# Attention and expert kernel: fp32 pairs scaled after the product instead of before, and one pair's scores in split halves

## The chip, the cores and the metric

One NeuronCore of a Trainium2 chip runs the whole program. The metric is the device time of one execution in microseconds; the median over the timed runs is compared. Engines: PE multiplies matrices, DVE (VectorE), ACT (ScalarE) and POOL (GpSimd) do element-wise work, SP (SyncE) issues the DMAs.

## What is computed

```python
q_pool = q.reshape(B, H, S // 2, 2, D).mean(axis=3)        # B=4, H=8, S=1152, D=64
scores = (q_pool @ k^T) / sqrt(D);  scores -= max(scores)
attn = exp(scores);  attn = attn / (sum(attn) + 1e-9)
x = attn @ v                                                # then (2304, 512)
h = x @ w_in;  g = where(h > 0, h, exp(min(h, 0)) - 1)
out = g @ w_out                                             # w_in 512x2048, w_out 2048x512
```

All inputs and the output are fp32.

## The kernel before

There are four units, one per batch entry. A unit has four pairs of heads. A pair is prepared once (q rows summed in twos, q and k transposed) and then runs nine steps: four blocks of 128 pooled queries for each head of the pair, and one step of 64 queries of both heads. A step makes 128 x 1152 scores on PE, takes their negated maximum on DVE while evicting them from PSUM into a buffer `ep` (`biggest`, L938), exponentiates in place on ACT with the row sum as a by-product (`expo`, L944), and makes the sum's reciprocal (`recip` on DVE, L952 and L953, or `recip_pool` on POOL, L960 and L961). After every second step, and after the last, the product with v gives a tile of x: five tiles per pair.

The string `SPLIT` names how each pair is computed, one letter per pair.

- `s`: scores and probabilities are split into fp16 halves. `phi` (ACT or POOL) and `plo` (DVE) multiply the exponentials by the reciprocal as they split them, DMAs transpose both halves, and 54 fp16 matmuls make a tile of x (`pv_split`, L1068).
- `F`: all fp32. q and k are transposed on PE (`flip`, L598 and L600, evicted at L603), scores are fp32 matmuls (`plain_rows`, L888 and L894). The exponentials are multiplied by the reciprocal in place, one pass over 128 x 1152 (L964 on POOL, L967 on DVE or L970 on ACT), transposed on PE in nine blocks (L1023), copied from PSUM to `pT` in three pieces (L1033 on ACT or L1036 on DVE), and 18 fp32 matmuls make a tile of x (`pv`, L1056).
- `f`: probabilities as in `F`, scores as in `s`: q and k go through absolute sums (L633), a scale (L685 to L689), a high half (L639 or, on POOL, L497), a low half (L653 or L659) and DMA transposes (L696 to L708); scores are fp16 matmuls (`whole_rows` and `half_rows`, L909, L914, L923).

Before, unit 0 is `FFFf`, units 1 and 3 are `ssss`, unit 2 is `ssfs`: five pairs have fp32 probabilities, 45 steps and 25 tiles of x. A tile of x is copied out of PSUM by L1077 (ACT) or L1081 and L1083 (DVE).

The experts follow each unit in two groups of 256 and 320 tokens: x is split into fp16 halves, 12 matmuls per block of `w_in` (L1167), the activation on ACT, DVE and POOL (L1180 to L1229), 12 matmuls per block of `w_out` (L1248). The weights arrive as raw words, are decoded on DVE (L776 to L780), summed on ACT (L792), and split (`split`: high half L803 or L497, low half L806 on DVE or L812 with L497 on POOL). That work falls into the time of unit 0.

The order of all 2,717 tasks is written out: `ORDER` lists them with a letter for the engine (p, v, a, g, s for PE, DVE, ACT, POOL, SP), each engine runs its own in that order, and `SLOTS` says which buffer each takes. PSUM has one buffer `s` of three banks for scores and five one-bank buffers `r` for everything else. `ep` has four buffers, in unit 0 joined by those of `wo` that are not yet in use.

Of the kernel before, what the change touches and what calls it, by code (L numbers as in the profile page):

```python
# [37 lines left out]
34s 509g 510g 493p 494v 472v 460a 33v 432p 433v 482p 461g 515p 495a 496v 483v 513p 42p 321v 530p
314s 473a 531v 497g 375s 514a 516a 293a 43a 309s 21a 306v 40p 44p 484a 462a 46p 511p 41a 485v 512a
48s 500p 310s 567p 501a 47a 568v 308a 299s 498p 517p 499a 569a 519p 486g 311v 474p 520v 45a 38p  # L40
467p 502p 475a 39a 316v 476p 570g 554p 521a 518a 555v 522g 523g 503a 487p 491p 477a 468a 36p 478p
465p 49g 479v 543p 456p 532a 533v 492a 488a 524p 323a 466a 534g 544v 545a 312v 50s 489p 463p 318a
578p 52a 546v 547g 490v 504p 53a 37a 324s 457v 464v 579v 54p 591p 535p 556a 557g 313a 301v 55v 592v
525a 552p 571g 539p 550p 536a 553a 548p 19s 537p 615p 51s 540a 326v 480p 616v 602p 580a 303a 328a
538a 558v 505v 617a 549a 528p 529a 551v 481v 559p 581g 329v 560a 56g 603v 618v 57g 561p 562a 582g
526p 330p 563p 604a 628p 61a 527v 331v 332p 377v 629v 583p 541p 605v 333v 584v 593a 594v 652p 390v
653v 58s 371s 62g 334g 619a 574p 564a 622p 587p 542a 379a 575a 630a 624p 620p 585p 586a 654a 639p
625v 572p 621a 335v 365s 360s 59s 588v 63s 336a 576p 565p 577a 623a 640v 60s 626p 663p 655v 367v
373v 641a 595a 566a 627a 606a 600p 337v 656v 631g 632g 381s 66s 64s 601a 573a 635p 636a 596p 607p
# [1272 lines left out]
```

## Time and profile before

| | |
|---|---|
| median of 3 runs | 751.39 us (751.33 to 752.59) |
| the profiled execution | 749.68 us, its span 747.8 us |
| busy: PE, DVE, ACT, POOL | 97%, 83%, 78%, 48% of the span |
| granted TensorE clock | 0.999 |
| DMA queue with the transfers | 83% of 16 engines, 125.49 MB |

The span runs from the first to the last instruction; the execution's own time has what lies around it. Busy shares are averages over stages that differ: unit 0 with the weights up to some 160 us, a mixed stage, then attention of one unit beside the experts of the one before, and the last group of the experts alone.

### The profile page before, as it was taken

To read this page: it belongs to the slowest core of one execution; us is meant where nothing else is said; L and a number is where in the kernel's file an instruction comes from. 1 tells how busy PE (TensorE), PEld (TensorE's weight loads), DVE (VectorE), ACT (ScalarE), POOL (GpSimd) and SP (SyncE) were. 2 spreads that over 40 slices of the span, in tenths; PEclk is the share of its full clock that TensorE was granted. 3 is DMA by queue.
4 is the path that set the end of the run, shared out by engine and by line. 5 is a ranking of instruction groups with operands and counts; after the bars stand their busy time and mean duration, and the time that the engine had idled before them with its cause. 6 is when DMAs were issued, how large, how long until landed. Compare 5 with 4: busy or idle time off the path is not lost.

```text
span 747.8 us, 19687 instructions
## 1 busy us (share of the span) xinstructions
PE 722.1 (97%) x7900; PEld 479.3 (64%) x7900; DVE 623.8 (83%) x1077; ACT 583.6 (78%) x980; POOL 357.1 (48%) x404
## 2 busy tenths in 40 slices
PE   5999999998999999999999999999999999999997
PEld 3677776776556655685566566787566655865753
DVE  6999999999998879899888888999898879774340
ACT  3999999999889777787979778988868766753651
POOL 0145547457465646155363656444677431452330
PEclk9999999999999999999999999999999999999999
DMA  8754952749899999999999997899999999793001
GB/s 286 257 200 133 314 167 65 197 85 211 158 187 191 184 194 189 166 207 197 185 198 197 189 227 156 185 183 188 191 178 204 184 184 161 127 126 64 29 1 36
DMA packets 308299, 126.75 MB, mean 169 GB/s; under 512 B 282928, under 2 KB 284976, under 8 KB 308208
## 3 DMA queue, kind: packets, MB, share of 16 engines
q1 hardware_dynamic: 308208, 125.49, 83.0%
q8 instruction: 62, 1.02, 0.6%
q14 instruction: 29, 0.24, 0.1%
HBM read 45.09 MB, written 4.72 MB: 67 GB/s over the span
## 4 chain that ended last, share of the span: by engine, by line
PE 52%; DVE 5%; POOL 2%; issue 1%; ACT 1%; DMA 1%; SPq 0%; POOLq 0%; ACTq 0%; DVEq 0%
PE r L1248 17%; PE r L1167 17%; PE r L1068 7%; PE s L909 5%; PE s L923 3%; DVE ep L997 2%; PE r L1023 1%; PE r L1056 1%; DVE ep L938 1%; DMA pT<-ep 1%; PE s L914 1%; ACT ep L944 0%; DVE tmp L1203 0%; POOL hb L991 0%; DMA pT<-hb 0%
## 5 line engine op out<-in xcount | busy, mean ns | idle before, releaser
L1167 PE MATMUL r<-x,wi 128*128 128x256 f16 (+1 forms) x1536 | 197.9, 286 | 4.5 <-DVE tmp L1203 2.3
L944 ACT ACTIVATE ep<-ep,wk 128x1152 f32<-128x1152 f32 x137 | 171.4, 1252 | 31.3 <-DVE ep L938 30.2
L938 DVE TENSOR_SCALAR_CACHE_REDUCE ep<-s,sm 128x1152 f32<-128x1152 f32 x117 | 165.1, 1411 | 20.6 <-PE s L923 10.7
L1167 PEld LDWEIGHTS <-wi 128*128 128x128 f16 x1536 | 147.3, 98 | 47.9 <-issue 9.9
L1248 PE MATMUL r<-wo,g 128*128 128x512 f16 (+1 forms) x864 | 174.9, 380 | 0.2 <-POOL g L1221 0.2
L997 DVE SCALAR_TENSOR_TENSOR ep<-ep,wk,hb 128x1152 f16<-128x1152 f32 x99 | 145.7, 1475 | 9.4 <-ACT hb L994 5.0
L1248 PEld LDWEIGHTS <-g 128*128 128x128 f16 (+1 forms) x864 | 73.6, 100 | 83.3 <-issue 4.3
L991 POOL TENSOR_SCALAR hb<-ep,wk 128x1152 f16<-128x1152 f32 x47 | 64.5, 1373 | 63.8 <-DVE wk L953 35.1
L497 POOL TENSOR_SCALAR wk<-wk 128x1 f32<-128x1 f32 x72 | 28.6, 398 | 132.7 <-ACT ep L944 129.1
L1068 PEld LDWEIGHTS <-v 128*64 128x64 f16 x2970 | 77.9, 110 | 12.1 <-issue 11.3
L994 ACT ACTIVATE hb<-ep,wk 128x1152 f16<-128x1152 f32 x52 | 64.7, 1250 | 26.8 <-POOL wk L961 7.9
L1068 PE MATMUL r<-pT,v 128*64 128x128 f16 (+1 forms) x2970 | 85.0, 215 | 0.1
L909 PE MATMUL s<-kT,qT 128*128 128x512 f16 (+3 forms) x390 | 76.7, 327 | 3.1 <-DVE ep L938 3.1
L1221 POOL TENSOR_TENSOR g<-tmp,g 128x320 f16<-128x320 f32 (+1 forms) x61 | 67.5, 1114 | 20.3 <-ACT g L1217 19.2
L1203 DVE SCALAR_TENSOR_TENSOR tmp<-r,tmp 128x320 f32<-128x320 f32 (+1 forms) x96 | 52.3, 552 | 28.5 <-ACT tmp L1193 13.9
L1180 ACT ACTIVATE tmp<-r 128x320 f32<-128x320 f32 (+1 forms) x96 | 45.2, 478 | 32.0 <-PE r L1167 19.0
L1183 ACT ACTIVATE tmp<-tmp,us 128x320 f32<-128x320 f32 (+1 forms) x96 | 57.7, 610 | 1.7
L909 PEld LDWEIGHTS <-qT 128*128 128x128 f16 (+1 forms) x390 | 31.7, 100 | 33.8 <-issue 9.9
L1023 PE MATMUL r<-ident,ep 128*128 128x128 f32 x342 | 49.7, 281 | 2.6 <-POOL ep L964 1.5
L961 POOL TENSOR_TENSOR wk<-wk 128x1 f32<-128x1 f32 x72 | 46.0, 639 | 6.0
L1225 POOL TENSOR_SCALAR g<-tmp 128x320 f16<-128x320 f32 (+1 forms) x41 | 25.7, 631 | 46.5 <-DVE tmp L1203 26.6
L923 PE MATMUL s<-kT,qT 64*128 64x512 f16 (+1 forms) x260 | 45.9, 389 | 0.7 <-DVE ep L938 0.7
(152 smaller groups left out, 1075.5 us busy)
## 6 DMA issues: line engine op xcount, KB each, us to landing
k<-in_k_dram SPq DMA_DIRECT2D x16, 576.0 KB, 4.7
v<-in_v_dram SPq DMA_DIRECT2D x16, 576.0 KB, 4.6
q<-in_q_dram SPq DMA_DIRECT2D x16, 512.0 KB, 4.5
g<-in_moe_w_out_dram SPq DMA_DIRECT2D x16, 512.0 KB, 4.8
g<-in_moe_w_in_dram SPq DMA_DIRECT2D x14, 512.0 KB, 6.2
qT<-qT SPq DMA_DIRECT2D x39, 144.0 KB, 2.9
out_dram<-tmp SPq DMA_DIRECT2D x16, 256.0 KB, 3.1
pT<-hb SPq DMA_TRANSPOSE x99, 3.6
```

Source lines behind the costliest of these rows:

```text
L909: nc.tensor.matmul(s.ap[rows, c, 0:n], pr.qT.ap[:, 0, j, rows], keys[h][c], start=first[c], stop=not first[c] and c < 2, skip_group_check= ...
L923: nc.tensor.matmul(s.ap[rows, c, 0:512], pr.qT.ap[r, 1, j, rows], keys[h][c][r], start=first[c], stop=not first[c], skip_group_check=True,)
L938: nc.vector.tensor_scalar(e_(), s.ap.rearrange("p a b -> p (a b)")[:, 0:S], -0.5 / float(D) ** 0.5 if pr.plain else pr.sm.ap[:, 12:13], No ...
L944: nc.scalar.activation(out=e_(), in_=e_(), func=AF.Exp, bias=nm.ap[:, 0:1], scale=-1.0, accum_out=nm.ap[:, 1:2],)
L991: nc.gpsimd.tensor_scalar(hb.ap, e_(), nm.ap[:, 1:2], 1.0, op0=ALU.mult, op1=ALU.mult)
L994: nc.scalar.activation(out=hb.ap, in_=e_(), func=AF.Copy, scale=nm.ap[:, 1:2])
L997: nc.vector.scalar_tensor_tensor(out=e16(), in0=e_(), scalar=nm.ap[:, 1:2], in1=hb.ap, op0=ALU.mult, op1=ALU.subtract)
L1068: nc.tensor.matmul(half(h), pr.v16.ap[:, h, order[c], e], p, start=(j + c == 0), stop=(j == 2 and c == NCH - 1), skip_group_check=True,)
L1167: nc.tensor.matmul(hp.ap[:, f * n:(f + 1) * n], w_in16[g][:, a, c, (f0 + f) * 128:(f0 + f + 1) * 128], x16.ap[:, e, c, g0:g0 + n], start=( ...
L1183: nc.scalar.activation(out=en.ap[:, :m], in_=en.ap[:, :m], func=AF.Exp, scale=us.ap[:, 8:9])
L1221: nc.gpsimd.tensor_tensor(out=l, in0=gv, in1=h, op=ALU.subtract)
L1248: nc.tensor.matmul(op.ap[r0:r0 + tn, :], gt[qd].ap[:, a, fi, o:o + tn], w_out16(f // 2)[:, e, f % 2, :], start=(i < 128 // tn), stop=(i >= ...
```

## The change

In `F` and `f` pairs the pass that multiplies the exponentials by the reciprocal is gone; the transposes wait for the exponential alone. The reciprocals go into eight columns of their own (`rc`). After the product with v, two more fp32 matmuls per tile multiply the reciprocals, broadcast over 64 columns, with the identity, so that columns 128 onward of the same PSUM bank hold them along the free dimension. The tile of x is then made in two steps: the broadcast reciprocals are copied to the place of x (ACT or DVE), and DVE multiplies the product by them. The third pair of unit 0 (index 2, called the second pair with split scores) goes from `F` to `f`. `ORDER` (now 2,697 tasks) and `SLOTS` are made anew throughout; no two stretches of more than five tasks agree on any engine's list. The engine letters that differ in number, before to after: copies to `pT` ACT 104 to 116, DVE 31 to 19; weights' low halves DVE 14 to 10, POOL 2 to 6; activation's high halves (L1217, L1225) ACT 52 to 40, POOL 44 to 56; k's low halves POOL 4 to 6, DVE 9 to 8. Normalising passes before: ACT 22, POOL 20, DVE 3. Copies of the reciprocals after: ACT 17, DVE 8; copies of x in those pairs before: ACT 15, DVE 10.

```diff
...
-SPLIT = ("FFFf", "ssss", "ssfs", "ssss")
+SPLIT = ("FFff", "ssss", "ssfs", "ssss")
 
 
 class Port(float):
@@ -374,6 +375,7 @@
     pool("qT", 2, [128, 2, 9, 128], F16)
     pool("sm", 3, [128, 14], F32)
     plan.pool("nm", 5, lambda j: wk[:, 61 + 2 * j:63 + 2 * j])
+    plan.pool("rc", 8, lambda j: wk[:, 18 + j:19 + j])
     pool("ep", 4, [128, S], F32)
     pool("wo", NG // 2, [128, 4, 2, DM], F16)
     pool("pT", 2, [128, 2, NCH, 128], F32)
@@ -945,29 +947,25 @@
                 out=e_(), in_=e_(), func=AF.Exp, bias=nm.ap[:, 0:1], scale=-1.0, accum_out=nm.ap[:, 1:2],
             )
 
+        rc = nm if pr.split else plan.buf("rc")
+
         def recip():
+            d = nm.ap[:, 1:2]
             if pr.split:
-                ts(nc.vector, nm.ap[:, 1:2], nm.ap[:, 1:2], 2.0 ** -15, 1e-9 * 2.0 ** -15, op1=ALU.add)
+                ts(nc.vector, d, d, 2.0 ** -15, 1e-9 * 2.0 ** -15, op1=ALU.add)
+                nc.vector.reciprocal(d, d)
             else:
-                nc.vector.tensor_scalar(nm.ap[:, 1:2], nm.ap[:, 1:2], 1e-9, None, op0=ALU.add)
-            nc.vector.reciprocal(nm.ap[:, 1:2], nm.ap[:, 1:2])
+                nc.vector.tensor_scalar(d, d, 1e-9, None, op0=ALU.add)
+                nc.vector.reciprocal(rc.ap, d)
 
         def recip_pool():
             d = nm.ap[:, 1:2]
             if pr.split:
                 ts(nc.gpsimd, d, d, 2.0 ** -15, 1e-9 * 2.0 ** -15, op1=ALU.add)
+                nc.gpsimd.tensor_tensor(out=d, in0=d, in1=minus, op=ALU.pow)
             else:
                 ts(nc.gpsimd, d, d, 1e-9, 1.0, op0=ALU.add)
-            nc.gpsimd.tensor_tensor(out=d, in0=d, in1=minus, op=ALU.pow)
-
-        def norm_pool():
-            nc.gpsimd.tensor_scalar(e_(), e_(), nm.ap[:, 1:2], 1.0, op0=ALU.mult, op1=ALU.mult)
-
-        def norm_dve():
-            nc.vector.tensor_scalar(e_(), e_(), nm.ap[:, 1:2], None, op0=ALU.mult)
-
-        def norm_act():
-            nc.scalar.activation(out=e_(), in_=e_(), func=AF.Copy, scale=nm.ap[:, 1:2])
+                nc.gpsimd.tensor_tensor(out=rc.ap, in0=d, in1=minus, op=ALU.pow)
 
         n = 128 if st.h is not None else 64
         modes = ("row", "row") if pr.plain else ("full", "row")
@@ -976,12 +974,14 @@
                        modes=modes if st.h is not None else ("both" if pr.plain else "col", "both"))
         tm = plan.add("DVE", 1345.0, t0 - K("KM", u), biggest, [ts_] + pr.sc, [s, nm, ep] + ([pr.sm] if pr.sm else []), lag=45.0)
         te = plan.add("ACT", 1255.0, t0 - K("KE", u), expo, [tm], [nm, ep])
-        tr = plan.add("DVE", 262.0, t0 - K("KE", u), recip, [te], [nm], [("POOL", Port(200.0, 270.0), recip_pool)], lag=160.0)
+        tr = plan.add("DVE", 262.0, t0 - K("KE", u), recip, [te], [nm] if pr.split else [nm, rc], [("POOL", Port(200.0, 270.0), recip_pool)], lag=160.0)
         tr.pen = CFG["PENR"]
         if not st.h:
             pr.pT = plan.buf(*TTAGS[u.i])
-            pr.pt = []
-        pT = pr.pT
+            pr.pt, pr.rc, pr.rec = [], [], []
+        pr.rc.append(rc)
+        pr.rec.append(tr)
+        pT, rcs = pr.pT, pr.rc
         if pr.split:
             hb = plan.buf("hb")
             e16 = lambda: e_().bitcast(F16)[:, 0:S]
@@ -1012,10 +1012,6 @@
             pr.pt.append(plan.add("DMA", Move(1480.0, 1250.0, True), t0 - CFG["KC"], ptr(0), [th], [hb, pT], lag=450.0))
             pr.pt.append(plan.add("DMA", Move(1480.0, 1250.0, True), t0 - CFG["KC"], ptr(1), [tl], [ep, pT], lag=450.0))
         else:
-            th = plan.add("POOL", pol(S), t0 - K("KH", u), norm_pool, [tr], [ep, nm],
-                          [("DVE", Port(760.0), norm_dve), ("ACT", act(S), norm_act)])
-            th.pen = CFG["PENN"]
-
             for j in range(0, NCH, 3):
                 tp = plan.buf("r")
 
@@ -1035,7 +1031,7 @@
                 def out_dve(j=j, tp=tp):
                     nc.vector.tensor_copy(dst(j), tp.ap[:, 0:384])
 
-                tt = plan.add("PE", 335.0, t0 - K("KT", u) + j, turn, [th], [ep, tp, pT], lag=80.0)
+                tt = plan.add("PE", 335.0, t0 - K("KT", u) + j, turn, [te], [ep, tp, pT], lag=80.0)
                 tq = plan.add("ACT", 380.0, t0 - K("KL", u) + j, out_act, [tt], [tp, pT], [("DVE", 480.0, out_dve)])
                 tq.pen = CFG["PENT"]
                 pr.pt.append(tq)
@@ -1057,6 +1053,12 @@
                         half(h), pr.v32.ap[:, h, order[c]], p,
                         start=(c == 0), stop=(c == NCH - 1), skip_group_check=True,
                     )
+            for h in range(2):
+                cols = ident if st.h is not None else ident[:, 64 * h:64 * h + 64]
+                nc.tensor.matmul(
+                    x.ap[64 * h:64 * h + 64, 128:128 + n], rcs[h if st.h is not None else 0].ap.to_broadcast([128, 64]), cols,
+                    start=True, stop=True, skip_group_check=True,
+                )
 
         def pv_split():
             for j, (a, e) in enumerate(((0, 0), (0, 1), (1, 0))):
@@ -1074,19 +1076,30 @@
             return u.x32.ap[:, pr.p, st.t * 128:st.t * 128 + n]
 
         def xa():
-            nc.scalar.activation(out=xdst(), in_=x.ap[:, 0:n], func=AF.Copy, scale=pr.sm.ap[:, 13:14] if pr.split else 1.0)
+            nc.scalar.activation(out=xdst(), in_=x.ap[:, 0:n], func=AF.Copy, scale=pr.sm.ap[:, 13:14])
 
         def xb():
-            if pr.split:
-                nc.vector.tensor_scalar(xdst(), x.ap[:, 0:n], pr.sm.ap[:, 13:14], None, op0=ALU.mult)
-            else:
-                nc.vector.tensor_copy(xdst(), x.ap[:, 0:n])
+            nc.vector.tensor_scalar(xdst(), x.ap[:, 0:n], pr.sm.ap[:, 13:14], None, op0=ALU.mult)
+
+        def xmul():
+            nc.vector.tensor_tensor(out=xdst(), in0=x.ap[:, 0:n], in1=xdst(), op=ALU.mult)
+
+        def ra():
+            nc.scalar.activation(out=xdst(), in_=x.ap[:, 128:128 + n], func=AF.Copy)
+
+        def rb():
+            nc.vector.tensor_copy(xdst(), x.ap[:, 128:128 + n])
 
         vb = [pr.v16, pr.sm] if pr.split else [pr.v32]
-        tp = plan.add("PE", 27 * mm(n) + 25.0 if pr.split else 18 * (2.08 * n / 2.4 + 1.5), t0 + K("KV", u), pv_split if pr.split else pv,
-                      list(pr.pt) + pr.vdone, [x, pT, u.x32] + vb, modes=("col", "col"), lag=60.0)
-        u.xdone[0 if st.t < 2 else 1].append(plan.add("DVE", 230.0, t0 + K("KV", u) - K("KX", u), xb, [tp], [x, u.x32] + vb,
-                                                      [("ACT", 250.0, xa)]))
+        tp = plan.add("PE", 27 * mm(n) + 25.0 if pr.split else 18 * (2.08 * n / 2.4 + 1.5) + 1.7 * n, t0 + K("KV", u), pv_split if pr.split else pv,
+                      list(pr.pt) + pr.vdone + ([] if pr.split else pr.rec), [x, pT, u.x32] + vb + ([] if pr.split else rcs), modes=("col", "col"), lag=60.0)
+        kx, bx = t0 + K("KV", u) - K("KX", u), [x, u.x32] + vb
+        if pr.split:
+            tx = plan.add("DVE", 230.0, kx, xb, [tp], bx, [("ACT", 250.0, xa)])
+        else:
+            tb = plan.add("ACT", 250.0, kx, ra, [tp], bx, [("DVE", 230.0, rb)])
+            tx = plan.add("DVE", 250.0, kx, xmul, [tb], bx)
+        u.xdone[0 if st.t < 2 else 1].append(tx)
 
     for st in steps:
         plan.at = str(st.u.i)
```

## Rows read from the trace of the kernel before

**Rows 1.** Windows by stage: length, then busy time (instructions) of each engine.

```profile
core 0: us, PE busy (x) PEld busy (x) DVE busy (x) ACT busy (x) POOL busy (x), PEclk, DMA share, GB/s
...
20.00:160.00 140.00, 134.87 (x1384) 100.95 (x1382) 134.35 (x273) 134.99 (x253) 69.48 (x72) 1.00 0.57 175
160.00:310.00 150.00, 143.45 (x1649) 90.23 (x1645) 137.50 (x217) 122.97 (x196) 84.69 (x89) 1.00 1.03 185
310.00:692.00 382.00, 380.51 (x4468) 249.72 (x4467) 323.95 (x534) 294.22 (x475) 188.24 (x214) 1.00 0.97 177
```

**Rows 2.** The chain that ended last, its last pieces: start, length, what.

```profile
691.78 26.08 PE r L1167 x192
717.87 26.14 PE r L1248 x144
```

**Rows 3.** PE's waits from 20 to 160 us: total, times, longest.

```profile
PE r L1023 <- POOL ep L964: 1.5, 1, 1.5
PE s L888 <- DVE ep L938: 1.3, 1, 1.3
...
PE r L1167 <- DVE x L1083: 0.2, 1, 0.2
```

**Rows 4.** Timeline of PE in unit 0: start, length, what, count of records.

```profile
36.38 2.19 PE L1056 MATMUL r<-pT,v 128*64 128x128 f32 x36
38.50 1.13 PE L888 MATMUL s<-kT,qT 64*128 64x512 f32 x4
...
39.77 0.87 PE L1023 MATMUL r<-ident,ep 128*128 128x128 f32 x6
40.57 1.09 PE L600 MATMUL r<-ident,q 128*64 128x128 f32 x16
41.60 1.13 PE L888 MATMUL s<-kT,qT 64*128 64x512 f32 x4
...
42.88 0.44 PE L600 MATMUL r<-ident,k 128*64 128x128 f32 x4
43.15 1.26 PE L600 MATMUL r<-ident,q 128*64 128x128 f32 x20
44.34 0.87 PE L1023 MATMUL r<-ident,ep 128*128 128x128 f32 x6
```

**Rows 5.** Timeline of PE, one split step (L923 to L914), then the experts.

```profile
483.87 0.39 PE L923 MATMUL s<-kT,qT 64*128 64x512 f16 x2
...
484.75 2.78 PE L1167 MATMUL r<-x,wi 128*128 128x256 f16 x24
```

**Rows 6.** Groups by line: the normalising pass on three engines; busy us, mean ns.

```profile
L970 ACT ACTIVATE ep<-ep,wk 128x1152 f32<-128x1152 f32 x19 | 23.9, 1257 | 2.2 <-DVE wk L953 1.8
L964 POOL TENSOR_SCALAR ep<-ep,wk 128x1152 f32<-128x1152 f32 x17 | 22.2, 1305 | 12.1 <-ACT pT L1033 8.8 <-DVE wk L953 2.4
...
L967 DVE TENSOR_SCALAR ep<-ep,wk 128x1152 f32<-128x1152 f32 x2 | 1.6, 808 | 0.0
```

**Rows 7.** Groups by line: evictions and a weight's low half.

```profile
L1033 ACT ACTIVATE pT<-r 128x384 f32<-128x384 f32 x85 | 38.1, 493 | 2.9 <-PE r L1023 2.9
...
L1036 DVE COPY pT<-r 128x384 f32<-128x384 f32 x23 | 12.4, 549 | 0.3 <-PE r L1023 0.2
...
L806 DVE SCALAR_TENSOR_TENSOR wi<-wi,wk,wi 128x1024 f16<-128x1024 f32 x5 | 6.4, 1275 | 0.0
...
L1083 DVE COPY x<-r 128x128 f32<-128x128 f32 x10 | 2.8, 282 | 0.2 <-PE r L1056 0.2
```

**Rows 8.** Timeline of POOL near 295 us, two passes of one kind.

```profile
293.86 2.42 POOL L991 TENSOR_SCALAR hb<-ep,wk 128x1152 f16<-128x1152 f32 x1 [0.19 <-POOL wk L961]
...
297.82 1.23 POOL L991 TENSOR_SCALAR hb<-ep,wk 128x1152 f16<-128x1152 f32 x1 [0.64 <-DMA pT<-hb]
```

**Rows 9.** Timeline of DVE in the same stretch.

```profile
293.86 1.41 DVE L997 SCALAR_TENSOR_TENSOR ep<-ep,wk,hb 128x1152 f16<-128x1152 f32 x1
298.18 2.07 DVE L997 SCALAR_TENSOR_TENSOR ep<-ep,wk,hb 128x1152 f16<-128x1152 f32 x1
```

More of the change, by code (lines that the diff above doesn't have):

```diff
@@ L38 @@
[L38 to L49, printed above, removed]
@@ L186 @@
[L186 to L188 removed]
+2s 6p 7v 8p 0s 320s 305s 295s 9a 294s 1v 322v 12p 307v 13a 4p 420p 421v 5a 10p 11a 422a 423g 433p
+426p 427a 18s 297v 434v 289s 376s 296v 443p 444v 435a 428p 24p 25a 441p 14p 436g 429a 378v 410p
+319s 300s 325s 298a 411v 16s 445a 446g 291v 437p 438a 412a 466p 467v 451p 452a 327v 15a 418p 414p
@@ new lines @@
+1041v 1034g 1035v 1057v 1036s 1042a 1043v 1058a 1048p 145a 1059g 2032g 1049v 1037s 1011a 1028p
+1044s 143s 1066p 2010a 1060a 1061v 1050a 1051v 2011g 1052a 1067v 1045s 1062s 1029a 1054s 2036p
+1074p 1053v 1075v 2052v 1046p 1068a 2046p 1084p 1063s 1076a 1077v 1055s 2047p 2048p 1069g 1064p
+1070g 1072s 1078a 1906s 1080s 1071v 1085v 1092p 1079v 1073s 146a 1065v 1047a 1081s 2049a 1086a
+2053v 1087v 1088g 1090s 2037a 2038s 147p 2054p 2055v 2058a 2042p 2043a 2044s 1093v 2059v 1089v
+1102p 1091s 1094a 1095g 1096g 1103v 2056v 1098s 148v 1097v 1099s 2088p 2089a 2050v 2090a 1104a
@@ new lines @@
+2067p 1120p 2060p 149a 150v 151s 154a 2061a 1121v 155v 1105g 1106g 1107v 2051s 1138p 1139v 2062a
+2068a 2063a 2069a 1122a 2070g 159s 1082p 1100p 1108s 2071v 1123g 1124a 2057v 2064v 2065a 2091g
+2072g 1112p 1113v 2081p 1125v 1130p 2073g 1140a 1114a 2095p 1101v 1141v 2092v 2093a 1115v 1109s
+1126s 152s 1127s 161s 160v 2094v 1131v 1116a 1118s 156s 1083v 2066g 153s 1142g 1143v 2082a 2109p
+1110p 2096a 2083a 2084g 2097a 2098a 2085v 1117v 1111a 2110a 1148p 2111a 1132a 1133g 1149v 2099v
+1119s 1134g 2074p 2075a 2076a 2100g 2077g 2078v 2128v 1135v 1144s 162s 2102p 2122p 1166p 1167v
@@ new lines @@
+192v 1234a 2164p 1235v 2165a 2177g 2206p 2155a 1242a 2166a 1227s 1250a 2156v 2199p 2217v 2167v
+2168v 187v 2200a 2201a 2202v 2133v 1251v 2185p 2203v 1243g 1244g 2207a 2218a 1236s 2208a 2209a
+2219g 2210v 2192p 1245v 1237s 1258p 1252a 2144a 1259v 1238p 188s 194s 189s 1228p 2169a 2145a 2211a
+2212g 1229a 1253v 2186a 1239v 2187a 2170v 2193a 2194a 2146g 2204g 2205g 2147v 2148g 2188v 1266p
+1246s 2227p 1267v 2228a 1260a 2241p 2195g 2149g 2234p 2196v 2189v 2197a 2242a 1268a 1261g 1255s
+1254s 1276p 1247s 193s 2248p 1277v 1262g 2220p 1264s 1278a 2198g 2221a 2222a 1263v 2190g 2191v
@@ new lines @@
+1827p 2500a 1795g 2481s 2511p 1828v 1801a 2501v 2502a 1797s 1802g 1776v 1796v 2496v 1778s 1798s
+1829a 2512a 2513a 2504p 2514g 1830g 2503g 2505a 2506a 2532p 2519a 2507a 2508v 1803a 2515v 2525p
+1804v 1831a 2516g 1805s 2517g 2533a 1806s 1817p 1818v 2534a 2509g 1832v 2526a 2527a 2528g 1819a
+1779p 2510v 1833s 2520a 2521a 1780a 1781p 1782v 2529v 2546p 2547p 1820v 1821a 1834s 1835p 1822v
+1823s 1783a 1807p 2535v 2536v 1784g 1785a 1824s 1787s 1809p 2552p 2553p 1836a 2522v 1810v 2523a
+1811a 2539p 2487v 2537g 2540a 2530g 2531g 1812v 2538v 1808v 1813g 1815s 1814v 1816s 2541a 1786v
@@ new lines @@
+2524v 2542v 2548p 1788s 1825p 1826a 2559v 1789p 2543v 2544a 2545g 1790v 2558v 2554p 2560p 2561v
+2564a 2549p 2555p 2556a 2562v 2550a 2551s 2565v 2580p 2581a 2566p 2567a 2657p 2601p 2568a 2569g
+2570v 2571a 2557s 2563v 2582a 2587p 2583v 2584v 2602a 2603a 2572v 2585g 2586g 2588a 2589a 2590g
+2591v 2604g 2643p 2644a 2645a 2646a 2647v 2605v 2573p 2574a 2575a 2576g 2577v 2578g 2579v 2664p
+2665a 2636p 2666a 2592g 2593v 2606g 2607g 2615p 2637a 2667a 2668v 2638a 2594p 2639g 2640v 2648a
+2641g 2642g 2616a 2617a 2618g 2669a 2619v 2629p 2620g 2649g 2621v 2658a 2684p 2659a 2660v 2661v
```

266 lines of the change are left out of this document (122 added, 144 removed), and 84 rows, old and new, of the table SLOTS.

## The prediction

> **What bounds the kernel now.** I read the windows by stage first, because the busy shares of the whole span mix stages. From 310 us on PE is the bound: it is busy for 380.51 of 382 us, DVE for 323.95, and the 1.5 us left are all that any better order of the other engines could win there [rows 1]. The end of the chain says the same: the last group of the experts is 26.08 and 26.14 us of PE without a break [rows 2]; the change touches none of it. From 20 to 160 us it is different. PE is busy for 134.87, DVE for 134.35 and ACT for 134.99 of 140 us: three engines at 96%, so none of them alone is the bound, and a relief of one runs into the next within some 5 us. From 160 to 310 us PE has 6.55 us idle, DVE 12.5, ACT 27 [rows 1]. So outside the start the whole idle time of PE that a lighter DVE or ACT can give back is 5.1 + 6.6 = 11.7 us before 310 us, and 1.5 after. PE's waits in the first stretch name the work that the change removes only for 1.5 us (the normalising pass on POOL); 1.3 us more wait for the eviction of scores on a full DVE [rows 3].
>
> **The change on PE.** An fp32 score step runs from 41.60 to 42.88 us, 1.28 us; a split step from 483.87 to 484.75 us, 0.88 us [rows 4, 5]. Nine steps of the third pair: 9 x 0.40 = 3.6 us saved. Its transposes go too: q takes 1.03 us (40.57 to 41.60) and 1.19 us (43.15 to 44.34), k's odd block 0.27 us (42.88 to 43.15), and eight square blocks at 0.13 us (six took from 39.77 to 40.57) 1.1 us: 3.6 us [rows 4]. One small matmul for the absolute sums comes in, at most 0.2 us. So this pair costs PE 7.0 us less. The broadcast of the reciprocals is new. Its two fp32 matmuls per tile have the shape of one of the nine column pairs in the product with v, which take 36.38 to 38.50 us, 2.12 us, for nine: 0.236 us a tile, half of that for the tile of 64. It could be nothing only if PE stood idle there; it could be 0.5 us if the two matmuls ran one after the other. I take 0.236: same type, same halves of the array, nothing between them. A pair has four whole tiles and a half one, 1.06 us; four such pairs in unit 0 cost 4.25 us, the one in unit 2 1.06 us [rows 4]. PE: -7.0 + 4.25 = -2.75 us in unit 0, +1.06 later, **-1.7 us** in all. Because PE has no slack after 310 us, this term should reach the end almost whole; its bounds are -3 and +5 us (broadcasts at 0.5 us: 25 x 0.26 = 6.5 us more).
>
> **The change on DVE and ACT, unit 0.** 36 of the 45 normalising passes lie in unit 0, by the table's letters 17 on ACT, 16 on POOL and 3 on DVE, at 1.257, 1.305 and 0.808 us [rows 6]. What the new table makes of it on DVE, by counting letters against rows: passes -3 x 0.81 = -2.4; copies to pT 21 to 8, -13 x 0.549 = -7.1; weights' low halves 14 to 10, -4 x 1.275 = -5.1 [rows 6, 7]. Against that 20 multiplications of 128x128 out of PSUM. No row shows one; a copy of that size is 0.282 us, a copy three times as wide 0.549 [rows 7], and I take 0.33, near the like size: +6.6. The third pair's low half of q and the fourth's, which moves from POOL, are passes of half the width of a weight's: +2 x 0.7; its scale chain is five tiny operations, +0.9; one copy of x fewer, -0.3; two low halves of the activation and one sum of q move away, -2. Sum -7.4 us, between -5 (multiplications at 0.45) and -9. ACT: -17 x 1.257 + 13 x 0.493 = -15, three passes more for the third pair (some 3.2), six evictions of transposes less (some -2.9): about -15 us [rows 6, 7]. POOL loses 16 passes, 21 us, and gets weights' and k's low halves; it is half idle, 69.48 of 140 us [rows 1], so its own length costs nothing while nobody waits for its results. Besides, each of the 36 steps loses the reciprocal and a pass of 0.8 to 1.3 us between the exponential and the transposes, so its `ep` buffer comes free earlier.
>
> **What that is worth.** The relief of DVE and ACT can only turn into time through PE's idle 11.7 us. Bounds: 0, where PE is idle for other reasons, and 7.4, what the busiest of the two loses. I take 3.0: the 1.5 us that name the removed pass, the 1.3 us that wait for a full DVE and the 0.2 us that wait for its copy of x [rows 3]. It lies below the middle because the three engines are level and PE's own order fills the gaps between its waits. What is late next is PE itself, and behind it the experts' evictions. After 310 us I take nothing: unit 2 loses nine passes on ACT and POOL, neither of which PE waits for there.
>
> **Waits that it adds.** The product with v now also waits for the reciprocals, with all later matmuls behind it on PE. They come a step of transposes and three copies (3 x 0.493 us) earlier [rows 7], and that covers them. The multiplication waits on DVE for ACT's copy, with score evictions behind it; if the copy is late, DVE stands for it. SP gets five issues more for the third pair (two transposes, three moves), with loads behind them; those are asked for tens of microseconds ahead in the table, and I cost them at nothing. Should that cover be gone, the decoding of weights is late and DVE with it.
>
> **Sum.** -1.7 - 3.0 = -4.7 us. Made against the profiled execution, 749.68 us (span 747.8, 1.9 us around it), it gives 745.0; the median of the runs shown, 751.39, lies 1.7 us above that execution, so the forecast for the median is **746.7 us**.
>
> **Rivals.**
>
> *PE alone.* The relief stays hidden because PE's idle time has other causes: only -1.7 us, 749.7 us. For it: three engines level, and most of PE's waits name DVE's evictions of scores, of which there are as many as before. Against it: DVE itself gets shorter.
>
> *The whole relief.* In unit 0 DVE is the true pace and PE only looks busy; its 7.4 us pass through: -9.1 us, 742.3 us. For it: DVE at 96%, and PE's records hide small gaps. Against it: ACT and PE at 96% as well.
>
> *POOL and DVE hold each other up.* A POOL pass of 1.23 us took 2.42 us when it began together with a DVE pass over two SBUF inputs, and that DVE pass took 2.07 instead of 1.41 us when POOL had begun 0.36 us before it [rows 8, 9]: the later one stands still for as long as the other runs. The change puts six more low halves on POOL, two passes each. If each of the 12 passes costs DVE the 0.66 us seen, that is 7.9 us, the relief is gone, and what is left is -1.7 and a little for the removed waits in one direction and late POOL results in the other: 750.2 us, no change that can be measured. Against it: 16 normalising passes that could do the same leave POOL in unit 0. The Trainium skill (SBUF — State Buffer, Who interferes with whom) says that DVE with two SBUF inputs and a POOL instruction that reads SBUF exclude each other for a whole instruction; the trace agrees. By that rule alone, moving a low half from DVE to POOL wins nothing, and the sum would be this rival's.
>
> *PSUM banks (slower).* A tile of x now leaves its `r` bank in two steps on two engines. The bank is held for the multiplication, 0.33 us, for the hand-over, and for what DVE has in hand when the copy is done: half of a pass of 1.41 us [rows 9], together about 1.0 us more. There are five such banks, and the transposes, the expert matmuls and the products all need them. If PE waits 0.3 us of it per tile, 25 x 0.3 = 7.5 us: 746.7 + 7.5 = 754.2 us, slower. It decides from about (4.7 + 1.5) / 25 = 0.25 us per tile on. For it: PE fills a bank in 0.4 us with transposes, and DVE is full. Against it: in the first stretch PE waits for a copy of x out of its bank only once, for 0.2 us [rows 3], and the tables leave the planner free to put other work between.
>
> **How the numbers follow.** Forecast 0.40, PE alone 0.15, the whole relief 0.15, POOL against DVE 0.10, PSUM banks 0.20. A measurement of this kernel tells about 0.2% from no change, 1.5 us: below 749.9 us is faster, above 752.9 us slower. Faster: 0.40 + 0.15 + half of PE alone (it lies on the line) = 0.63. Same: the other half and most of POOL against DVE, 0.16. Slower: the banks and a rest, 0.21. The forecast's own range is 743.5 to 749.8 us. Eight in ten needs the other cases: down to 741.5, a little past the whole relief, up to 754.5, the price of the banks.
>
> **What the profile after would show.** PE's busy time about 2 us less, the broadcast at 0.24 us a tile, the third pair's steps at 0.88 us. DVE some 7 us and ACT some 15 us less busy before 310 us; windows from 20 to 160 us with DVE and ACT below 96% and PE at or above it. The first experts (L1167, L1248) of unit 0 two to five microseconds earlier, and the stage after 310 us as long as before. Wrong would be: PE waits for copies or multiplications of x, for banks, or for POOL's low halves of weights; SP waits that delay loads in the first 80 us; or PE idle after 310 us beyond 1.5 us, which new tables could bring anywhere.

## The result, and the profile after

The changed kernel takes **756.49 us** (median of 9 runs, 753.19 to 757.24), the kernel before 751.33 beside it (9 runs, 749.62 to 753.51): ratio 1.0062, 95% interval 1.0044 to 1.0081. It is slower by 5.2 us where I forecast 4.7 us faster; 756.49 lies above the top of my range, 754.5. The profiled execution took 757.17 us, its span 755.4. It lies 7.5 us above the profiled one before, more than the medians do, so the losses read from the two profiles below add up to more than 5.2 us.

Windows by stage after, to be held against [rows 1]; the last two lines look closer at two short stretches with PE alone:

```profile
20.00:160.00 140.00, 128.97 (x1367) 99.61 (x1366) 132.40 (x266) 120.46 (x243) 58.65 (x62) 0.96 0.62 181
160.00:310.00 150.00, 144.72 (x1629) 91.59 (x1627) 135.18 (x218) 121.28 (x191) 91.22 (x91) 1.00 0.99 179
310.00:692.00 382.00, 376.88 (x4515) 249.11 (x4514) 328.42 (x546) 280.38 (x459) 184.53 (x223) 1.00 0.98 179
...
104.00:120.00 16.00, 12.11 (x107) 0.79 0.25 92
140.00:155.00 15.00, 11.80 (x109) 0.89 0.25 75
```

ACT lost what I said (14.5 us in the first stage), POOL 10.8. DVE lost only 2.0 and PE is idle for 11.0 of 140 us instead of 5.1. The granted clock, 1.00 before, is 0.96: behind 104 and behind 140 us it fell to the lower of its two levels (1.2 instead of 2.4 GHz) for a while: 0.51 from 107 to 114 us, 0.50 from 144.6 to 148. After 310 us PE is idle for 5.1 us instead of 1.5. The fp32 products of unit 0 end at 171.0 us (before 166.8), those of unit 2 at 492.0 (483.9), the last split product at 691.5 (683.9): some 4 us are lost up to 171 us, some 4 between there and 492, nothing after.

PE's waits from 20 to 160 us after, against [rows 3]:

```profile
PE s L925 <- DVE ep L940: 4.7, 2, 3.9
PE r L1019 <- DVE x L1085: 3.2, 1, 3.2
PE s L890 <- DVE ep L940: 1.4, 2, 1.2
```

Two long waits, both for DVE, make up the new idle time. The first, in the timeline of DVE (L778, L779 and L782 are the three operations of a decoding, L940 the eviction of scores):

```profile
99.93 1.60 DVE L493 TENSOR_SCALAR sm<-sm 128x3 int32<-128x3 int32 x1
...
102.65 0.41 DVE L778 TENSOR_SCALAR tmp<-g 128x512 uint32<-128x512 uint32 x1
103.10 1.49 DVE L779 SCALAR_TENSOR_TENSOR tmp<-g,tmp 128x512 uint32<-128x512 uint32 x1
104.62 2.49 DVE L782 SCALAR_TENSOR_TENSOR wo<-g,tmp 128x512 uint32<-128x512 uint32 x1
107.04 1.41 DVE L940 TENSOR_SCALAR_CACHE_REDUCE ep<-s,sm 128x1152 f32<-128x1152 f32 x1
```

and in that of POOL and of PE:

```profile
99.36 2.15 POOL L814 TENSOR_TENSOR wi<-wi,wi 128x1024 f16<-128x1024 f32 x1
102.79 1.26 POOL L499 TENSOR_SCALAR wi<-wi,wk 128x1024 f32<-128x1024 f32 x1 [1.28 <-ACT wi L805]
104.13 2.44 POOL L814 TENSOR_TENSOR wi<-wi,wi 128x1024 f16<-128x1024 f32 x1
```

```profile
104.23 0.39 PE L1058 MATMUL r<-ident,wk 128*64 128x128 f32 x4
108.51 0.61 PE L925 MATMUL s<-kT,qT 64*128 64x512 f16 x2 [3.89 <-DVE ep L940]
```

The operation at 99.93 is three columns wide and takes 1.60 us; the one behind it of the same form takes 0.17. It ends when POOL's pass at 99.36 ends. The decoding's second and third operations take 1.49 and 2.49 us where 0.69 is usual, beside two more passes of POOL. These are low halves of the input weights. The new table moved the one at 99.36 to POOL; the one at 102.79 and 104.13 (task 341) ran on POOL before, too, and it is the new order that puts a decoding beside it. The eviction that PE needs is queued behind the decoding. The second wait has the same make-up: between 140.0 and 144.1 us a high half of v and a sum of q on POOL hold two decodings up, and the multiplication of a tile of x, whose bank PE wants, stands behind them:

```profile
140.01 1.23 POOL L499 TENSOR_SCALAR v<-v,sm 128x1152 f16<-128x1152 f32 x1 [2.85 <-PE r L1052]
140.19 1.60 DVE L782 SCALAR_TENSOR_TENSOR wo<-g,tmp 128x512 uint32<-128x512 uint32 x1
...
142.50 1.60 POOL L579 TENSOR_TENSOR q<-q 128x576 f32<-128x576 f32 x1
142.88 1.77 DVE L782 SCALAR_TENSOR_TENSOR g<-g,tmp 128x512 uint32<-128x512 uint32 x1
144.58 0.41 DVE L1085 TENSOR_TENSOR x<-r,x 128x128 f32<-128x128 f32 x2
```

The Trainium skill (SBUF — State Buffer, Who interferes with whom) says that of a DVE operation with two SBUF inputs and a POOL instruction that reads SBUF, the one that starts first keeps the shared ports for its whole instruction. The decodings at 103.10 and 104.62 agree: each began behind a pass of POOL and ended 0.54 us behind that pass's end.

To see how much DVE loses that way, I count its operations from 20 to 172 us that took over 0.4 us longer than the median of their line and shape in the same run, and call them held: three in the kernel before, 2.3 us too long in all; ten in the kernel after, 11.7 us. Beside each of them POOL had a pass in hand. Five of the ten, 6.2 us, lie beside low halves of weights, the other five beside POOL's passes on q, k, v and the probabilities.

### The profile page after: what moved, and what is told of

It is laid out like the page before. It is cut to its first block, busy times and chain, and to the rows that moved or that the text cites. A ratio compares the mean times of both kernels' runs of the same rounds, so it can differ in the third digit from the quotient of the medians.

```text
span 755.4 us, 19764 instructions
## 1 busy us (share of the span) xinstructions
PE 722.4 (96%) x7953; PEld 481.9 (64%) x7953; DVE 627.0 (83%) x1087; ACT 554.4 (73%) x952; POOL 354.8 (47%) x413
## 5 line engine op out<-in xcount | busy, mean ns | idle before, releaser
L940 DVE TENSOR_SCALAR_CACHE_REDUCE ep<-s,sm 128x1152 f32<-128x1152 f32 x123 | 173.7, 1412 | 23.4 <-PE s L925 15.0
L991 POOL TENSOR_SCALAR hb<-ep,wk 128x1152 f16<-128x1152 f32 x50 | 67.7, 1354 | 53.6 <-DVE wk L956 20.5
L499 POOL TENSOR_SCALAR wk<-wk 128x1 f32<-128x1 f32 x70 | 19.5, 279 | 154.9 <-ACT ep L946 151.1
L911 PE MATMUL s<-kT,qT 128*128 128x512 f16 (+3 forms) x420 | 83.1, 328 | 4.6 <-DVE ep L940 4.6
L1070 PEld LDWEIGHTS <-v 128*64 128x64 f16 x2970 | 77.8, 110 | 12.4 <-issue 11.7
L994 ACT ACTIVATE hb<-ep,wk 128x1152 f16<-128x1152 f32 x49 | 61.1, 1249 | 25.0 <-POOL wk L965 11.3
L1234 POOL TENSOR_TENSOR g<-tmp,g 128x320 f16<-128x320 f32 (+1 forms) x57 | 62.1, 1092 | 22.5 <-ACT g L1230 20.6
L911 PEld LDWEIGHTS <-qT 128*128 128x128 f16 (+1 forms) x420 | 33.9, 100 | 37.9 <-issue 15.0
L925 PE MATMUL s<-kT,qT 64*128 64x512 f16 (+1 forms) x280 | 49.6, 390 | 7.1 <-DVE ep L940 7.1
L1238 POOL TENSOR_SCALAR g<-tmp 128x320 f16<-128x320 f32 (+1 forms) x54 | 40.5, 754 | 32.5 <-DVE tmp L1216 28.6
L1201 POOL TENSOR_SCALAR tmp<-tmp,us 128x320 f32<-128x320 f32 (+1 forms) x39 | 29.9, 768 | 52.4 <-ACT tmp L1196 51.1
```

The lines of the kernel that those rows point to most:

```text
L911: nc.tensor.matmul(s.ap[rows, c, 0:n], pr.qT.ap[:, 0, j, rows], keys[h][c], start=first[c], stop=not first[c] and c < 2, skip_group_check= ...
L925: nc.tensor.matmul(s.ap[rows, c, 0:512], pr.qT.ap[r, 1, j, rows], keys[h][c][r], start=first[c], stop=not first[c], skip_group_check=True,)
L940: nc.vector.tensor_scalar(e_(), s.ap.rearrange("p a b -> p (a b)")[:, 0:S], -0.5 / float(D) ** 0.5 if pr.plain else pr.sm.ap[:, 12:13], No ...
L991: nc.gpsimd.tensor_scalar(hb.ap, e_(), nm.ap[:, 1:2], 1.0, op0=ALU.mult, op1=ALU.mult)
L994: nc.scalar.activation(out=hb.ap, in_=e_(), func=AF.Copy, scale=nm.ap[:, 1:2])
L1070: nc.tensor.matmul(half(h), pr.v16.ap[:, h, order[c], e], p, start=(j + c == 0), stop=(j == 2 and c == NCH - 1), skip_group_check=True,)
```

## The experiments

All were timed in five rounds, each beside the kernel before on the same chip (its medians: 750.07 to 751.52 us). Where two kernels of different experiments are compared I take the difference of their ratios to the kernel before, times 750 us, with the root of the sum of the squared half intervals as its uncertainty; by its ratio the kernel after stands at +4.7 us. Line numbers of the experiments differ by up to two from those of the kernel they come from. In ORDER, a number is a task, the letter its engine.

**1. Low halves back on DVE, decodings later, both** (from the kernel after).

```diff
-335g 339g 341g 345g 347g        # e1: low halves of five blocks of w_in
+335v 339v 341v 345v 347v
-357v 387v ... 770v              # e2: two decodings behind a multiplication of x; e3: both edits
+770v 357v 387v
```

> The changed kernel with the five low halves of w_in that POOL makes put back on DVE, at the same places of the list. Theory A (POOL's low halves hold DVE up; PE then stands still and its clock falls): the long DVE passes between 99 and 107 us are gone, with them PE's wait of 3.9 us at 104.6 us and the stretch of half clock behind it (5.4 us of work at half speed, 2.7 us lost): some 5 to 7 us less than the changed kernel, 749 to 751 us, although DVE gets 5 x 1.27 = 6.4 us of work of its own. Theory B (the tile of x made in two steps, with its PSUM bank held, costs the time): no gain, or slower by what DVE gets, 756 to 760 us.

> The changed kernel with two multiplications of x (third pair) put ahead of two weight decodings on DVE's list; nothing else moves. Theory B: PE's wait of 3.2 us at 145 us for the bank that such a multiplication frees is gone, and 3.2 us at half clock behind it (1.6 us lost): 4 to 5 us less, about 752 us. Theory A: DVE is late there because POOL held two of its decodings up (1.60 and 1.77 instead of 0.69 us), so the wait moves to the next user of DVE; at most 1 us less, 755 to 757 us.

> Both edits. If the two stalls are separate, their gains add: 10 to 12 us less than the changed kernel, 745 to 747 us, under the kernel before. If they are one (DVE late all along), the sum is no more than the larger one: 749 to 752 us. Theory C (what is lost after 310 us by the new order, some 3.5 us, is a third cause): not below 747 us.

Measured: 756.18, 757.29 and 755.05 us (ratios 1.0060, 1.0078 and 1.0051; each interval holds 1.0062). In e1 the operations at 99 to 107 us run at their usual length and DVE's held time falls from 11.7 to 5.4 us, but the five low halves (one of them had been on POOL before the change) cost DVE as much, 5 x 1.275 us, and PE stands for 3.8 us at the second place, not 3.2. In e2 PE's second wait becomes one of 4.0 us for a score eviction. Both together win 0.8 us (uncertain by 1.8); a wait of 3.7 us at 146 us is left. So a stall removed by more work on DVE comes back at the next user of a late DVE.

**2. The mirror: four more low halves on POOL in the kernel before.**

```diff
-335v 339v 345v 347v
+335g 339g 345g 347g
```

> The kernel before, with four of the low halves of w_in that DVE makes put on POOL at the same places (six of eight then run there). Theory A: DVE loses 5.1 us of work but stands still for POOL's passes, and late weights come on top: 2 to 8 us slower, 753 to 759 us. Theory B, and the step of the forecast that counted the move as a relief of DVE: same or up to 3 us faster, 748 to 752 us.

Measured 757.82 us, ratio 1.0084 (1.0067 to 1.0102): 6.3 us slower, with this one part of the new table, in the old order. DVE's decodings from 20 to 172 us, in this run:

```profile
L776 DVE SCALAR_TENSOR_TENSOR tmp<-g,tmp 128x512 uint32<-128x512 uint32 x26 | 22.4, 862 | 0.9
...
L779 DVE SCALAR_TENSOR_TENSOR wo<-g,tmp 128x512 uint32<-128x512 uint32 x14 | 11.4, 814 | 0.5
```

in the kernel before:

```profile
L777 DVE SCALAR_TENSOR_TENSOR tmp<-g,tmp 128x512 uint32<-128x512 uint32 x27 | 19.5, 724 | 0.9
...
L780 DVE SCALAR_TENSOR_TENSOR wo<-g,tmp 128x512 uint32<-128x512 uint32 x14 | 9.7, 692 | 0.5
```

and in the kernel after:

```profile
L782 DVE SCALAR_TENSOR_TENSOR wo<-g,tmp 128x512 uint32<-128x512 uint32 x14 | 13.2, 943 | 0.5
...
L782 DVE SCALAR_TENSOR_TENSOR g<-g,tmp 128x512 uint32<-128x512 uint32 x2 | 2.5, 1230 | 0.1
```

The same operations on the same data sizes: 26 x 0.138 + 14 x 0.122 = 5.3 us longer in e8, and 14 x 0.251 + 2 x 0.54 = 4.6 us longer in the kernel after. About as much DVE time is lost there as the move was to save (5.1 us). With DVE's other operations, e8 has eleven held ones, 9.1 us, 6.9 more than before: the move costs DVE more than it saves.

**3. The change on the order of the kernel before.** e4 moves the scaling and nothing else, e5 also moves 16 copies to `pT` from DVE to ACT, e6 is the whole change, e7 is e6 with e5's move.

```diff
-... recip, norm, turn ...    pv, x (a or v)
+... recip, turn ...          pv, xr (a or v; e5, e7: v), xmul v
```

> The kernel before with the scaling moved and nothing else: its order of tasks, its engines and its third pair in whole fp32; the 45 normalising passes are left out, each fp32 tile of x gets the broadcast, the copy of the reciprocals on the engine that copied x before, and the multiplication on DVE right behind it. PE: 20 whole and 5 half broadcasts at 0.31 and 0.16 us, +7.0 us. DVE in unit 0: 20 multiplications at 0.28 and 3 passes of 0.81 fewer, +3.2 us. New tables guilty: this order has few late score evictions, so only PE's 7 us less some idle time that goes away: 756 to 758 us. Scaling itself guilty (the two-step way out of the bank holds up PE in any order, 0.2 us a tile more): 761 us or more, with PE waits on the multiplication of x of over 4 us between 20 and 160 us. Forecast's own terms (broadcast 0.236, relief 3): 754.

> As e4_scale_only, but the copies of the reciprocals on DVE and 16 copies to pT of unit 0 moved from DVE to ACT, which lost 17 passes: DVE's sum in unit 0 falls by 16 x 0.55 less the copies that came to it. If a full DVE is what holds PE up in unit 0: 2 to 4 us faster than e4_scale_only. If the bank is what holds PE (the copy and the multiplication now follow each other on one engine, so without a hand-over): also faster, and PE's waits on x near 0 in both. If PE alone sets the time: equal to e4_scale_only within 1 us.

> The whole change on the order of the kernel before: moved scaling as in e4_scale_only, and the third pair with split scores, its new tasks put where the old flips stood. New tables guilty: e4_scale_only less the third pair's 7 us of PE, give or take 2 for DVE's two more passes: 749 to 753 us, 3 to 7 us faster than the kernel after. Structure guilty, in any order: 755 to 758 us, as the kernel after.

> The whole change on the order of the kernel before, with the copies of the reciprocals on DVE and 16 copies to pT of unit 0 moved from DVE to ACT. New tables guilty and DVE the pace of unit 0: the forecast's relief shows here, 746 to 750 us, faster than the kernel before. Structure guilty: 754 us or more. PE alone the bound: equal to e6_before_order within 1 us.

Measured: 765.87, 767.68, 772.38 and 776.58 us (ratios 1.0193, 1.0219, 1.0286 and 1.0337), 8 us (e4) to 27 us (e7) above what the theory of guilty tables gave, and in e4 without the waits on the multiplication that the other one asked for. In e4 DVE is busy for only 126.47 us of the first stage's 140, and PE is idle for 9.4; 5.3 us of its waits name late score evictions. A lighter DVE alone won nothing in this order, which was written for other lengths, and moving 16 copies off it made it no better (e5 against e4 2.0 us slower, uncertain by 2.5; e7 against e6 3.8 by 2.8). The third pair's change made it 7.0 us slower here (e6 against e4), where PE was to save as much; PE waits 3.1 us there for one absolute sum of q that ACT makes, so this says little of the new order, in which no run tests the third pair alone. So "the new tables are to blame, the old order would do better" falls: the new tables serve the change far better than the old order does. What hurts in them has to be looked for inside the new order.

**4. What PE's broadcasts cost.** e9 makes them in 16 bits, e11 issues them twice.

```diff
-rcs[h ...].ap.to_broadcast([128, 64]), cols
+rcs[h ...].ap.bitcast(BF16)[:, 1:2].to_broadcast([128, 64]), cols      # e9, cols likewise
-for h in range(2):
+for h in (0, 1, 0, 1):                                               # e11
```

> The kernel after with the broadcast's two matmuls in 16 bits: they read the upper 16 bits of the reciprocal and of the identity, so each reciprocal is cut to 8 bits of mantissa; order, engines, waits and every other instruction as they were. A broadcast took 0.31 us in fp32; in 16 bits I expect about a quarter, 0.08. If PE sets the time wherever the broadcasts lie: 25 tiles x 0.2 = 5 us less, 751.5 us, as fast as the kernel before. If late DVE work sets the pace of unit 0 and of unit 2's pair: PE arrives earlier and waits longer, 755 to 756.5 us.

> The kernel after with the broadcast's two matmuls issued twice into the same place, nothing else. If PE sets the time: 25 more broadcasts at 0.28 to 0.31 us, +7 us, 763.5 us. If PE's idle time in unit 0 and in unit 2's pair takes them in: +1 to +3 us, 758 to 759.5 us.

Measured: e9 755.51 us (ratio 1.0077, 1.0057 to 1.0096), no faster than the kernel after (1.1 us slower, uncertain by 2.0), with a broadcast at 0.16 us (100.64 to 100.80 us) instead of 0.32 and the granted clock in the two short stretches as in the kernel after; e11 **753.32** (1.0044, 1.0029 to 1.0059), where +7 or +1 to +3 us were expected: 25 more broadcasts cost nothing, and the middle value is 1.4 us lower (uncertain by 1.8). Less work on PE wins nothing at the same clock, and more costs nothing, so the amount of PE's work isn't the pace of unit 0. In e11 the second broadcasts shorten the two waits to 3.2 and 1.5 us (the one at 104.23 us above is the last thing PE does before the first), and the granted clock from 104 to 120 us is 0.89 instead of 0.79, from 140 to 155 us 1.00 instead of 0.89. That suggests that the clock gives back what the work costs.

**5. That reading tested: PE kept busy in the two stalls only.**

```diff
-for h in range(2):
+for h in (0, 1) * (8 if (u.i, pr.p) == (0, 2) and st.t in (0, 4) else 1):
```

> The kernel after with two tiles' broadcasts issued eight times into the same place: the whole tile that ends at 104.6 us, right ahead of PE's 3.9 us of waiting, and the tile of 64 that ends at 139.9, three tasks ahead of the 3.2 us. PE gets 7 x 0.31 + 7 x 0.16 = 3.3 us more to do, all in place of standing idle. If the half clock behind the two stalls is part of the loss: the granted clock stays near full from 104 to 150 us and the time falls, 753 to 754.5 us. If the clock costs nothing there because DVE sets the pace: 756 to 757. If PE's work counts: 759.

Measured **753.39 us** (1.0030, 1.0015 to 1.0046): 2.4 us gained (uncertain by 1.8) with 3.3 us more work. The two stretches, PE alone:

```profile
104.00:120.00 16.00, 13.62 (x153) 0.89 0.30 113
140.00:155.00 15.00, 12.62 (x142) 1.00 0.24 75
```

Against 0.79 and 0.89 in the kernel after. So the slower clock behind the two stalls is a part of the loss, about half by the middle value; the waits themselves stay, 2.4 us each, and so does DVE's held time, 11.4 us. The executions of the kernel after agree: the two with a mean granted clock of 0.997 took 753.19 and 754.39 us, the seven with 0.992 or 0.993 took 755.39 to 757.24.

**6. The multiplications' DVE time.**

```diff
-nc.vector.tensor_tensor(out=xdst(), in0=x.ap[:, 0:n], in1=xdst(), op=ALU.mult)
+nc.vector.tensor_tensor(out=xdst()[:, 0:1], in0=x.ap[:, 0:1], in1=xdst()[:, 0:1], op=ALU.mult)
```

> The kernel after with the 25 multiplications cut to one column of the tile (the rest of x keeps the reciprocals, so the results are not scaled): same tasks, order, hand-over and waits, but about 0.1 us instead of 0.28 and half as much for a tile of 64; 4.3 us less DVE work, 3.5 of it in unit 0. If DVE's load in unit 0 sets the time: 752 to 753 us. If the wait for a late place in DVE's queue does, not the work: 755.5 to 756.5 us.

Measured 753.88 us (1.0041, 1.0027 to 1.0056), 1.6 us less (uncertain by 1.8); a multiplication now took 0.149 us instead of 0.281, or instead of 0.208 for a half tile. For the 15 whole and 4 half ones up to 172 us that is 15 x 0.132 + 4 x 0.059 = 2.2 us of DVE time. The size fits a DVE that sets the pace; the interval doesn't prove it.

**7. POOL's second pass, and the control.** e15 takes it out of the kernel after, e17 out of the kernel before.

```diff
-ts(nc.gpsimd, x(), x(), c, 1.0)
-nc.gpsimd.tensor_tensor(out=to()[:, 1], in0=x(), in1=to()[:, 0], op=ALU.subtract)
+ts(nc.gpsimd, to()[:, 1], x(), c, 1.0)
```

> The kernel after with the weights' low halves on POOL in one pass with one input instead of two passes (the low half then holds the scaled weight and not the remainder). DVE keeps its own. If POOL's passes are what makes DVE late: the stretched decodings at 99 to 107 and 135 to 145 us go, DVE gains 3 to 5 us without more work, 751.5 to 753 us. If they only move the loss, as e1_lo_dve did: 755.5 to 756.5 us.

> The kernel before with the edit of e15_lo_one_pass: its two low halves on POOL (it has six after the change) in one pass with one input, so that they hold the scaled weight and not the remainder. If the 8 us that the edit was worth in the kernel after come from the four low halves more that the new table puts on POOL: about 2/6 of it or less here, 748.5 to 750.5 us. If they are worth as much in any table: 744 us or less.

Measured: e15 **748.51 us** (0.9964, 0.9949 to 0.9978), 7.4 us less than the kernel after (uncertain by 1.8) and faster than the kernel before. Its first stage:

```profile
20.00:160.00 140.00, 133.42 (x1467) 102.77 (x1468) 134.95 (x283) 127.68 (x257) 56.09 (x63) 1.00 0.64 187
```

Clock at 1.00, no wait of PE in it above 1.2 us, DVE's held time 5.7 us, the fp32 products of unit 0 done by 163.8 us. A part of the gain may come from the work that it leaves out. The control didn't behave: e17 took 753.97 us (1.0040, 1.0022 to 1.0057), 3.0 us *slower* than before, though POOL does less. Its decodings:

```profile
L777 DVE SCALAR_TENSOR_TENSOR tmp<-g,tmp 128x512 uint32<-128x512 uint32 x26 | 20.7, 797 | 0.9
...
L780 DVE SCALAR_TENSOR_TENSOR wo<-g,tmp 128x512 uint32<-128x512 uint32 x14 | 10.5, 749 | 0.5
```

26 x 0.073 + 14 x 0.057 = 2.7 us more than in the kernel before: with everything on POOL at other moments, its remaining passes met other DVE operations. (Its profile has a stretch at the lower clock level from 15 to 25 us, mean 0.66, and so has that of e8. But the four executions of e17 with a mean clock of 0.998 or more took 753.85 to 754.75 us, and the two of e8 with 0.998 took 757.57 and 758.41, so that stretch isn't what made them slow.) So what counts is not how long POOL works alone, but also what its passes run beside. It follows that e17 can't say how much of e15's 7.4 us belongs to the four low halves more; and as an edit that only lightens POOL moved the old order by 3.0 us, e8's 6.3 us may hold a shift of that size, too.

**8. Long passes or much time.** The same results in pieces.

```diff
+for j in range(nch):
+    ts(nc.gpsimd, x()[:, j], x()[:, j], c, 1.0)
+    nc.gpsimd.tensor_tensor(out=to()[:, 1, j], in0=x()[:, j], in1=to()[:, 0, j], op=ALU.subtract)
```

> The kernel after with each low half on POOL computed in four pieces (two for the output weights), two short passes each, the same result. If it is the length of one pass that makes DVE late (2.1 to 2.4 us in one go): the decodings at 99 to 107 us are stretched less, 752 to 754 us. If it is POOL's whole time on two inputs, which the pieces do not shorten: 755.5 to 758 us.

Measured **751.84 us** (1.0006, 0.9989 to 1.0023), 4.2 us less than the kernel after (uncertain by 1.9): the loss in time is gone, with the whole computation done and POOL's subtractions longer in sum (20 x 0.730 + 2 x 1.157 = 16.9 us; after 11.3 + 2.1). DVE at the first place now:

```profile
103.06 0.56 DVE L778 TENSOR_SCALAR tmp<-g 128x512 uint32<-128x512 uint32 x1
103.65 0.85 DVE L779 SCALAR_TENSOR_TENSOR tmp<-g,tmp 128x512 uint32<-128x512 uint32 x1
104.53 1.05 DVE L782 SCALAR_TENSOR_TENSOR wo<-g,tmp 128x512 uint32<-128x512 uint32 x1
105.50 1.41 DVE L941 TENSOR_SCALAR_CACHE_REDUCE ep<-s,sm 128x1152 f32<-128x1152 f32 x1
```

None of them takes half a microsecond more than usual, and the eviction starts 1.5 us earlier. The decodings as a whole are as long as in the kernel after (the groups with `tmp`, `wo` and `g` 35.2 us against 35.3), but the long holds have become few: five, 4.6 us, instead of ten, 11.7. The longest is left where POOL makes a low half of k, which this edit doesn't cut:

```profile
114.46 1.51 DVE L779 SCALAR_TENSOR_TENSOR tmp<-g,tmp 128x512 uint32<-128x512 uint32 x1
...
115.52 2.69 POOL L661 TENSOR_TENSOR kn<-k,kn 128x1152 f16<-128x1152 f32 x1
116.00 2.75 DVE L782 SCALAR_TENSOR_TENSOR wo<-g,tmp 128x512 uint32<-128x512 uint32 x1
...
120.14 0.68 PE L912 MATMUL s<-kT,qT 128*64 128x512 f16 x6 [2.65 <-DVE ep L941]
```

Behind it PE stands for 2.65 us, and the granted clock, 1.00 from 104 to 120 us, is 0.66 from 120 to 125. From 20 to 160 us PE is idle for as long as in the kernel after (10.5 us against 11.0), in shorter pieces and with a clock of 0.99 instead of 0.96. Of the versions with the full computation it is the best; it equals the kernel before and doesn't beat it.

**9. Unit 2, and sums of mends.** e10 moves 23 tasks of 310 to 490 us off DVE, e12 is e10 with e3, e16 is e3 with the broadcasts of unit 0 twice.

```diff
-2139v 2167v 2202v 2188v 2237v ... 2108v 2115v 2156v ...
+2139a 2167a 2202a 2188a 2237a ... 2108g 2115g 2156g ...
```

> The kernel after with 23 tasks of the stretch from 310 to 490 us taken off DVE and put on ACT (five ELU passes, six copies of x or of reciprocals, five copies to pT) or POOL (seven low halves of g), order unchanged; some 12 us off DVE's 159 of 180. If DVE's load there makes the score evictions late: PE's 3.5 us idle between 320 and 500 us go to under 1, 753 us. If it is the order (the eviction is queued behind work that is late itself): PE's idle time stays within 1 us of 3.5, 756 us.

> e10_u2_relief together with e3_both (five low halves of the input weights on DVE, two decodings behind the multiplications). Theories as there: if each removes its own share, 755.05 - 3 = 752 us; if PE only meets the next late eviction, 755.

> e3_both, that is five low halves on DVE and two decodings behind the multiplications, with the broadcasts of unit 0 issued twice as in e11_bc_twice. If the mended order (1.4 us) and the kept clock (3 us) add up: 751 to 752 us. If they mend the same loss: 753 to 755 us.

Measured: 762.44, 762.10 and 755.38 us (ratios 1.0159, 1.0163 and 1.0061). Windows from 310 to 500 us, in e10:

```profile
310.00:500.00 190.00, 182.13 (x2189) 120.66 (x2189) 154.98 (x247) 143.50 (x249) 104.43 (x125) 1.00 0.97 184
```

in the kernel after:

```profile
310.00:500.00 190.00, 186.49 (x2251) 125.11 (x2249) 168.35 (x285) 141.10 (x238) 99.26 (x122) 1.00 1.03 190
```

and before:

```profile
310.00:500.00 190.00, 189.77 (x2229) 127.31 (x2228) 165.01 (x270) 160.96 (x262) 95.09 (x114) 1.00 1.02 192
```

With 13 us less on DVE PE is idle for 7.9 us instead of 3.5: its waits still name score evictions, and some name ACT now. So less load on DVE alone doesn't mend unit 2. The edit is no clean test, as it puts seven passes more on POOL and 16 on ACT. Held operations don't tell the kernels apart there: six, 4.1 us, from 310 to 500 us before and after alike, eight, 5.5 us, in e10. The sequence of the tasks may be the cause; I couldn't single it out. e16 shows that the mends of unit 0 don't add up.

## Why the prediction was wrong

**The failed step** is in "The change on DVE and ACT, unit 0": weights' low halves "14 to 10, -4 x 1.275 = -5.1" counted as relief, with POOL's length that "costs nothing while nobody waits for its results". DVE itself waits, operation by operation: its held time grew from 2.3 to 11.7 us, which takes back the 5.1 and more, and as several holds come in one place the stall reaches PE. With the long holds cut to 4.6 us at the same order and the same results (e18) the loss is gone. Not all of it comes from the halves that were moved: 3.6 of the 11.7 us lie beside them, 2.6 beside the low half that was on POOL before, 5.5 beside other passes of POOL, so the new order has its share in what lies beside what. I had this mechanism as a rival ("POOL and DVE hold each other up") and priced it at 7.9 us of DVE's time, where 9.4 us came; but I gave it 0.10 and let it only cancel the relief.

**A price that no step had:** the slower clock behind a stall, 2.4 us in e13 (uncertain by 1.8). With it a held-up DVE ends on the slow side, not at "no change".

**PE.** The sum of -1.7 was of no use in unit 0. The broadcast takes 0.32 us (100.27 to 100.59 us), not 0.236. But by e9 halving that wins nothing (uncertain by 2.0), and by e11 doubling it costs nothing. The third pair's split steps take 0.88 us as foreseen.

**What it is worth.** My 3.0 us of relief didn't come. The terms listed for DVE add up to -8.0 us, not to the -7.4 that stands there; that shifts only the whole relief, by 0.6 us. Whether 3.0 is the right size without the holds stays open: e18, the best with the whole computation, only equals the kernel before, and e15 (0.9964, 2.7 us faster than before) leaves work out.

**"After 310 us I take nothing"** failed too: 3.5 us idle between 310 and 500 us against 0.2, and much the same in all ten versions that keep this part of the new order (PE busy for 186.26 to 187.65 us of 190). Its cause stays open; e10 only shows that taking load off DVE in this way doesn't mend it.

**PSUM banks**, the slower rival, came nearest in time (754.2), but not by its mechanism: from 20 to 160 us PE waited for a multiplication once, for 3.2 us, not 0.3 us a tile, and behind held-up decodings. That its number came near was luck.

**Right:** ACT's 15 us; the multiplication, nearly (taken at 0.33, measured at 0.281); the last stage unchanged.
